# An attention pair on one core: the softmax guard from Gram matrices, and linear attention's K and V as separate jobs

## The chip, the cores and the metric

The kernel runs on one core of one Trainium2 chip. The metric is the device time of one execution in microseconds (us), as the median of several runs; the kernel before was run three times. The profile is of one execution, and its span (761.9 us) is a little shorter than that run's device time (764.1 us).

Engine names in the profile: PE is the matrix engine's multiplications, PEld its weight loads, DVE the vector engine, ACT the scalar engine (which evaluates the exponential), POOL the general-purpose engine, SP the engine that here only issues transfers. L833 is line 833 of the kernel.

## The reference

Two attention blocks with 2048 tokens, width 512 and 32 heads of 16 are computed side by side, each with its own input and weights. A is linear attention, B is full softmax attention. Their outputs are concatenated. All inputs are bf16, drawn from a normal distribution and scaled by 0.05.

```python
qkv = (x @ wqkv).reshape(B, S, 3, H, Dh).transpose(2, 0, 3, 1, 4)   # H = 32, Dh = 16
# A:
phi = lambda t: jnp.where(t > 0, t + 1, jnp.exp(t)) + 1e-6
pq, pk = phi(q), phi(k)
kv  = jnp.einsum("bhsd,bhse->bhde", pk, v);  z = jnp.einsum("bhsd->bhd", pk)
num = jnp.einsum("bhqd,bhde->bhqe", pq, kv)
den = jnp.einsum("bhqd,bhd->bhq", pq, z)[..., None] + 1e-6
a   = (num / den).transpose(0, 2, 1, 3).reshape(B, S, D) @ wo
# B:
scores = jnp.einsum("bhqd,bhkd->bhqk", q, k) * Dh ** -0.5
b   = einsum("bhqk,bhkd->bhqd", softmax(scores), v).transpose(0, 2, 1, 3).reshape(B, S, D) @ wo
out = concatenate([a, b], axis=-1)
```

The exponentials of B are the bulk: 32 heads x 2048 x 2048 scores. The kernel cuts them into 2048 blocks of 128 keys x 512 queries of one head; a block is a tile of 128 partitions x 512 columns.

## The kernel before

Softmax is computed without subtracting a row maximum. A guard bounds the largest score. Only if the bound exceeds a threshold does a second, general program run at the end; with these inputs it does not.

Each score block takes one of two ways. On the ACT way, PE writes three or two blocks into the score banks (`SCR`, tile pS), and one ACT instruction of 1536 or 1024 columns takes the exponential into PT. On the DVE way, PE writes one block into one of the two remaining banks (`DB`, tile pD), DVE turns it into an int16 whose bits are an approximate power of two (tile DI), and for three blocks at a time three more DVE instructions refine it into two factors (DQ and DI). PE then multiplies the exponentials with V and accumulates in pPV: one multiplication for an ACT block, two for a DVE block. 64 blocks (16 key tiles x 4 heads) make a unit, and there are 32 units.

```python
def ex(st_, en_):                                       # the ACT way, w = 1536 or 1024 (L833)
    sch.add("act", lambda e: e.activation(PT[:, row, c0:c0 + w], SCR[sl][:, 0:w], ACTF.Exp, scale=SC), ...)

def p1(st_, en_, ...):                                  # the DVE way, one or two blocks (L773)
    sch.add("dve", lambda e: e.tensor_scalar(DI[:, buf, i * 512:(i + n) * 512], DB[:, bi * 512:(bi + n) * 512],
                                             ESC, EB, op0=ALU.mult, op1=ALU.add), ...)
ops = [                                                 # then, for a group of three (L889, L890, L891)
    (..., lambda e: e.tensor_scalar(Q, I, 0x3FF, 0x3800, op0=ALU.bitwise_and, op1=ALU.bitwise_or), ...),
    (..., lambda e: e.tensor_tensor(Qh, Ih, Qh, op=ALU.mult), ...),
    (..., lambda e: e.tensor_scalar(I, I, 0xFC00, 8, op0=ALU.bitwise_and, op1=ALU.bitwise_or), ...)]
```

Everything else (B's projections, all of A, the output projections) is cut into jobs. A job borrows one of the two DB banks for a PE part, followed by ACT or DVE parts that read that bank. The order of all instructions is fixed while the kernel is built: a planner keeps a clock for each engine and gives each instruction a planned length; whenever the plan shows DVE and a DB bank free, it sends a score block the DVE way, and the ACT way takes the rest. On the chip each engine then works through its list in that order and waits on semaphores.

```python
TEND = 755.0                          # the plan's assumed end; spreads B's and A's jobs over the time
def job_cand():                       # which job may start next
    bi = min((i for i in range(2) if dfree[i] is not None), key=lambda i: dfree[i], default=None)
    ...
    if j_.bank:
        if bi is None: continue       # no DB bank free
```

The parts that the change replaces, shortened:

```python
# guard: largest |q| and |k| of each projection (16 projections of Q, 16 of K)
("dve", 0.6, tensor_reduce(QMX[:, i:i+1], QT[:, r, cs], max, abs))              # L469, in each Q job, 128x512
("dve", 1.14, tensor_reduce(KMX[:, i:i+1], KM[:, r, :, cs], max, abs))          # L476, first K jobs, 128x1024
("dve", 0.6, tensor_reduce(KMX[:, i:i+1], KR[:, kr, :], max, abs))              # L490, other K jobs, 128x512
# bound_job: four small DVE instructions; flag_job: one small PE product and one DVE maximum into FLG

# A's exp part of phi: ACT exp into EA (L546), DVE min/add on EA (L547), DVE max/add with the bank (L549)
def akv_job(t, hp):                   # one token tile, half of the heads: K in columns 0:256, V in 256:512 of one bank
    st = halves(mm, ["Wa", ("xTa", t)], n=8, parts=2, dur=0.14)                 # 8 products of 256 columns
    st += phi_stages(0, 256, KNa[:, t, :], [("KNa", t)])                        # EA 256 wide
    st.append(("dve", 0.33, tensor_copy(VNa[:, t, :, 0:128], bank[:, 256:512])))   # L559
```

Of the kernel before, what the change touches and what calls it, by code (L numbers as in the profile page):

```python
# [123 lines left out]
THRESHOLD_BITS = 0x41140000  # L124
# [99 lines left out]
def bass_concat_heads__linear_attn_block__softmax_full_mha__prompt_kernel(nc, A_x, A_wqkv, A_wo, B_x, B_wqkv, B_wo, out):  # L224
# [3 lines left out]
    NGP = 4  # L228
# [15 lines left out]
    TEND = 755.0  # L244
# [3 lines left out]
    FM = 0.12  # L248
    WARM = (30,)
# [8 lines left out]
    with es:  # L258
# [38 lines left out]
        QMX = sb("QMX", [128, NGP * NC], F32)  # L297
        KMX = sb("KMX", [128, NGP * NC], F32)
        BND = sb("BND", [128, NGP], F32)
        BN1 = sb("BN1", [128, 1], F32)  # L300
# [99 lines left out]
        def push(eng, ready, prio, dur, run):  # L400
            seq[0] += 1
            cands[eng].append((ready, prio, seq[0], dur, run))

        class Job:
# [11 lines left out]
            def stage_done(self, i, end, bk, bi):  # L416
                if i == self.rel and bi is not None:
                    dfree[bi] = end + LAT
                for st, tk in self.gives:
                    if st == i:  # L420
                        tok[tk] = end + LAT
                if i + 1 < len(self.stages):
                    eng, dur, fn = self.stages[i + 1]
                    lat = LAT if eng != "pe" or eng != self.stages[i][0] else 0.0
                    push(eng, end + lat, self.prio if eng == "pe" else (0 if i + 1 <= self.rel and self.bank else min(self.prio, 2)), dur,
                         lambda st_, en_, fn=fn: (fn(bk), self.stage_done(i + 1, en_, bk, bi)))
# [29 lines left out]
        def proj_job(Gp, sc, kind, fast=False, **kw):  # L456
# [10 lines left out]
            if kind == 0:  # L467
                st.append(("dve", 0.6, f_ev("dve", lambda e, bk: e.tensor_copy(QT[:, r, cs], f32v(bk)), [], [("QT", r, sc)])))
                st.append(("dve", 0.6, f_op("dve", lambda e: e.tensor_reduce(QMX[:, i:i + 1], QT[:, r, cs], axis=AX.X, op=ALU.max,  # L469
                                                                             apply_absolute_value=True), [("QT", r, sc)], [("QMX", i)])))  # L470
                return Job(st, needs, [(2, ("Q", Gp, sc)), (3, ("QMX", i))], rel=2, **kw)
            if fast:
                for e_ in range(2):
                    st.append(("dve", 0.67, f_ev("dve", lambda e, bk, e_=e_: e.tensor_scalar(KM[:, r, e_, cs], f32v(bk), PAR[:, e_:e_ + 1], None, op0=ALU.mult),
                                                 [("PAR", e_)], km_keys(r, e_, sc))))
                st.append(("dve", 1.14, f_op("dve", lambda e: e.tensor_reduce(KMX[:, i:i + 1], KM[:, r, :, cs], axis=AX.XY, op=ALU.max,  # L476
                                                                            apply_absolute_value=True),
                                            km_keys(r, 0, sc) + km_keys(r, 1, sc), [("KMX", i)])))
                return Job(st, needs, [(2, ("K", Gp, 0, sc)), (3, ("K", Gp, 1, sc)), (4, ("KMX", i))], rel=3, **kw)
# [3 lines left out]
            def spread(bk):  # L483
                for e_ in range(2):
                    for g in range(4):
# [4 lines left out]
            st.append(("dve", 0.6, f_op("dve", lambda e: e.tensor_reduce(KMX[:, i:i + 1], KR[:, kr, :], axis=AX.X, op=ALU.max,  # L490
                                                                         apply_absolute_value=True), [("KR", kr)], [("KMX", i)])))
            return Job(st, needs, [(3, ("K", Gp, 0, sc)), (3, ("K", Gp, 1, sc)), (4, ("KMX", i))], rel=2, **kw)

        def bound_job(**kw):
            n = NGP * NC
            return Job([
                ("dve", 0.2, f_op("dve", lambda e: e.tensor_reduce(BND[:, 0:NGP], QMX[:].rearrange("p (g s) -> p g s", s=NC), axis=AX.X, op=ALU.max),
                                  [("QMX", i) for i in range(n)], ["BND"])),
                ("dve", 0.2, f_op("dve", lambda e: e.tensor_reduce(KMX[:, 0:NGP], KMX[:].rearrange("p (g s) -> p g s", s=NC), axis=AX.X, op=ALU.max),
                                  [("KMX", i) for i in range(n)], [("KMX", i) for i in range(n)])),  # L500
                ("dve", 0.2, f_op("dve", lambda e: e.scalar_tensor_tensor(BND[:], BND[:], SC, KMX[:, 0:NGP], op0=ALU.mult, op1=ALU.mult),
                                  ["BND"] + [("KMX", i) for i in range(n)], ["BND"])),
                ("dve", 0.2, f_op("dve", lambda e: e.tensor_reduce(BN1[:], BND[:], axis=AX.X, op=ALU.max), ["BND"], ["BN1"])),
            ], [("QMX", i) for i in range(n)] + [("KMX", i) for i in range(n)], [(3, "BN1")], bank=False, **kw)

        def flag_job(**kw):
            return Job([
                ("pe", 0.3, f_pe(lambda e, bk: e.matmul(bk[0][0:1, bk[2]:bk[2] + 128], lhsT=BN1[:], rhs=BMk[:], start=True, stop=True), ["BN1", "BMk"])),
                ("dve", 0.3, f_ev("dve", lambda e, bk: e.tensor_reduce(FLG[:], bk[0][0:1, bk[2]:bk[2] + 128], axis=AX.X, op=ALU.max), [], ["FLG"]))],
                ["BN1"], [], **kw)  # L510

# [40 lines left out]
        def akv_job(t, hp, **kw):  # L552
            def mm(e, bk, i):
                k_, cc = divmod(i, 4)
                return e.matmul(f32v(bk)[:, 256 * k_:256 * k_ + 256], lhsT=xTa[:, cc, t * 128:(t + 1) * 128],  # L555
                                rhs=Wa[:, cc, 512 + 512 * k_ + 256 * hp:512 + 512 * k_ + 256 * hp + 256], start=(cc == 0), stop=(cc == 3))
            st = halves(mm, ["Wa", ("xTa", t)], n=8, parts=2, dur=0.14)
            st += phi_stages(0, 256, KNa[:, t, :], [("KNa", t)])
            st.append(("dve", 0.33, f_ev("dve", lambda e, bk: e.tensor_copy(VNa[:, t, :, 0:128], f32v(bk)[:, 256:512].rearrange("p (b n) -> p b n", n=128)),  # L559
                                        [], [("VNa", t)])))  # L560
            return Job(st, [("xTa", t)] + ([("akv", hp - 1, bl) for bl in range(2)] if hp else []),
                       [(5, ("ak", hp, t))], **kw)

        def akvsum_job(hp, bl, **kw):
# [7 lines left out]
            return Job(st, [("ak", hp, t) for t in range(NT)], [(3, ("akv", hp, bl)), (5, ("rha", bq))], **kw)  # L572
# [120 lines left out]

        afree = [0.0, 0.0]
# [16 lines left out]
        def d_backlog(at):  # L711

            w = max(0.0, T["dve"] - at) + sum(c_[3] for c_ in cands["dve"])
            for s_ in dgroup["st"].values():
                if not s_.get("chained"):
                    w += 1.0 * len(s_["items"])
# [27 lines left out]
        def d_take(pk):  # L744
# [3 lines left out]
            if not dgroup["open"]:  # L748
# [4 lines left out]
                dgroup["st"][buf] = {"p1": 0, "closed": False, "items": []}  # L753
            s_ = dgroup["st"][buf]
            i = len(s_["items"])
            s_["items"].append(b)
            dgleft[buf] += 1
            if len(s_["items"]) == DG:
                s_["closed"] = True
                dgroup["open"] = False  # L760
            return b, buf, bi, i

        def d_emit(tk, en):

            for b, buf, bi, i in tk:
                bk = DBANK[bi]
                sch.add("pe", lambda e, bk=bk, b=b: qk(e, f32v(bk), b), reads=qk_reads([b]), writes=[bk[3]])
            pair = len(tk) == 2 and tk[0][1] == tk[1][1] and tk[0][2] == 0 and tk[1][2] == 1
            for part in ([tk] if pair else [[x] for x in tk]):
                n = len(part)  # L770
                _, buf, bi, i = part[0]
                def p1(st_, en_, part=part, n=n, buf=buf, bi=bi, i=i):
                    sch.add("dve", lambda e: e.tensor_scalar(DI[:, buf, i * 512:(i + n) * 512], DB[:, bi * 512:(bi + n) * 512],  # L773
                                                             ESC, EB, op0=ALU.mult, op1=ALU.add),
                            reads=[("D", bi + x) for x in range(n)], writes=[("DI", buf, i + x) for x in range(n)])
                    for x in range(n):
                        dfree[bi + x] = en_ + LAT
                    s_ = dgroup["st"][buf]
                    s_["p1"] += n
                    s_["t"] = en_  # L780
                    chain(buf)
                push("dve", en + LAT, 0, 0.065 + 0.535 * n, p1)
# [3 lines left out]
        def fill_act_cand():  # L786
# [19 lines left out]
            def run(st, en):  # L806
# [16 lines left out]
                if tk:  # L823
                    tk.sort(key=lambda x: x[3])
# [16 lines left out]
        def fill_d_cand():  # L841
# [11 lines left out]
            def run(st, en):  # L853
# [4 lines left out]
                tk.sort(key=lambda x: x[3])  # L858
# [9 lines left out]
        def chain(buf):  # L868
            s_ = dgroup["st"][buf]
            if not s_["closed"] or s_["p1"] < len(s_["items"]):  # L870
# [213 lines left out]
        for e_ in range(2):  # L1084
            for j, t_ in enumerate((6.6, 8.5, 9.3)):
# [5 lines left out]
        kmx = ("dve", 1.14, f_op("dve", lambda e: e.tensor_reduce(KMX[:, 0:1], KM[:, 0, :, 0:512], axis=AX.XY, op=ALU.max, apply_absolute_value=True),  # L1091
                                 km_keys(0, 0, 0) + km_keys(0, 1, 0), [("KMX", 0)]))
        qmx = ("dve", 0.6, f_op("dve", lambda e: e.tensor_reduce(QMX[:, 0:1], QT[:, 0, 0:512], axis=AX.X, op=ALU.max, apply_absolute_value=True),
                                [("QT0", i) for i in range(2)], [("QMX", 0)]))
        urgent, urgent2, early, bjobs, ajobs = [], [], [], [], []
        urgent2.append(Job([kmx], gives=[(0, ("KMX", 0))], bank=False, ready=30.0))
        urgent2.append(Job([qmx], gives=[(0, ("QMX", 0))], bank=False, ready=30.0))

# [16 lines left out]
        bjobs.append(bound_job(ready=0))  # L1115
        bjobs.append(flag_job(ready=0))
        aout_job = lambda t: omm_job("a", t, 4 + t % 2, [("aont", t)], [(1, ("aout", t))])
        for hp in range(2):
            for t in range(NT):
                ajobs.append(akv_job(t, hp))  # L1120
# [15 lines left out]
        def job_cand():  # L1136
            best = None
            bi = min((i for i in range(2) if dfree[i] is not None), key=lambda i: dfree[i], default=None)
            for lst, pr in ((urgent, 0.5), (early, 2), (bjobs, 2.2), (urgent2, 2.3), (ajobs, 2.5)):
                for pos, j_ in enumerate(lst[:1] if lst is not urgent2 else lst[:8]):  # L1140
# [4 lines left out]
                    if j_.bank:  # L1145
                        if bi is None:
# [3 lines left out]
                    if best is None or (st, pr) < (best[0], best[1]):  # L1150
                        def run(st_, en_, j_=j_, lst=lst, fn=fn):
                            lst.remove(j_)
                            bk, b_ = (DBANK[bi], bi) if j_.bank else (None, None)
                            if j_.bank:
                                dfree[bi] = None
                            fn(bk)
# [164 lines left out]
```

## Time and profile before

| | |
|---|---|
| device time, median of 3 | 765.7 us (764.09 to 766.62) |
| span of the profiled execution | 761.9 us |
| ACT busy | 745.3 us (98%), 695 instructions |
| DVE busy | 721.9 us (95%), 1287 instructions |
| PE busy | 688.9 us (90%), of which 114.3 us products of L1181 that only fill pauses |
| PE clock granted, mean | 0.997 of full speed |
| blocks on the ACT way / the DVE way | 1603 / 445 |

The counts of blocks are those of the products into pS and pD on L682. "Busy" is the time in which at least one instruction of an engine is under way; since the end of one instruction overlaps the start of the next, counts times mean length come to more than the busy time. The planner's lengths in the code are assumptions of the kernel's author, and no measurement.

### The profile page before, as it was taken

What the parts mean: (1) busy time and instruction counts of PE and PEld (TensorE: products, weight loads), DVE (VectorE), ACT (ScalarE), POOL (GpSimd) and SP (SyncE); (2) the same over time, 40 slices, a digit from 0 to 9 for tenths busy, and PEclk for the clock granted to TensorE, in tenths of its full rate; (3) what the DMA queues carried; (4) which work ended last, traced back from release to release, by engine and by line L of the source; (5) the groups of instructions that cost most, each with busy time, mean ns of one, the idle gap of its engine ahead of it and who ended that gap; (6) DMA issues with size and microseconds to landing.
All of it is one profiled execution on the core that took longest, in us unless ns stands there. A gap on an engine that the chain in (4) does not pass through costs nothing.

```text
span 761.9 us, 14767 instructions
## 1 busy us (share of the span) xinstructions
PE 688.9 (90%) x6181; PEld 238.0 (31%) x6232; DVE 721.9 (95%) x1287; ACT 745.3 (98%) x695; POOL 8.6 (1%) x27
## 2 busy tenths in 40 slices
PE   8889999998999998999888899998998989899896
PEld 4223333333333333333222333222323232223232
DVE  5999979999999999999999999999999999999993
ACT  6999999999999999999999999999999999999995
POOL 4000000000000000000000000000000000000000
PEclk9999999999999999999999999999999999999999
DMA  9900000000000000000010000000010001010001
GB/s 216 226 1 2 1 1 8 15 9 2 1 1 2 1 1 2 9 14 8 22 22 8 1 10 21 22 19 11 16 28 15 9 1 43 22 36 22 22 8 33
DMA packets 36570, 17.29 MB, mean 23 GB/s; under 512 B 27536, under 2 KB 35984, under 8 KB 36496
## 3 DMA queue, kind: packets, MB, share of 16 engines
q1 hardware_dynamic: 35408, 15.61, 8.4%
q8 instruction: 51, 0.84, 0.5%
q10 hardware_dynamic: 1088, 0.66, 0.3%
q14 instruction: 23, 0.19, 0.1%
HBM read 4.46 MB, written 4.19 MB: 11 GB/s over the span
## 4 chain that ended last, share of the span: by engine, by line
ACT 96%; PE 2%; DMA 1%; SPq 0%; issue 0%; DVE 0%; DVEq 0%; ACTq 0%
ACT PT L833 94%; ACT EA L546 2%; DMA Wb<-in_B_wqkv_dram 1%; PE pS L1013 0%; PE pPV L1181 0%; PE pS L682 0%; PE pPV L961 0%; SPq L332 0%; ACT KNa L440 0%; PE pS L1055 0%; PE pD L1055 0%; DVEq L1265 0%; DVE DI L773 0%; PE pD L1181 0%; PE pD L576 0%
## 5 line engine op out<-in xcount | busy, mean ns | idle before, releaser
L833 ACT ACTIVATE PT<-pS 128x1536 f16<-128x1536 f32 (+1 forms) x641 | 740.0, 1488 | 1.8 <-PE pS L682 1.0
L773 DVE TENSOR_SCALAR DI<-pD 128x512 int16<-128x512 f32 (+1 forms) x435 | 296.6, 694 | 10.0 <-PE pD L682 8.0
L682 PE MATMUL pS<-QT,KM 32*128 32x512 bf16 x1603 | 249.9, 385 | 49.3 <-ACT PT L833 36.1
L961 PE MATMUL pPV<-PT,VV 128*17 128x512 f16 x1603 | 209.8, 383 | 0.7 <-ACT PT L833 0.7
L682 PE MATMUL pD<-QT,KM 32*128 32x512 bf16 x445 | 161.1, 385 | 1.0 <-DVE PQT L549 0.6
L682 PEld LDWEIGHTS pS<-QT,KM 32*128 32x128 bf16 x1603 | 61.2, 91 | 272.9 <-ACT PT L833 257.8
L890 DVE TENSOR_TENSOR DQ<-DI,DQ 128x1536 f16<-128x1536 f16 x149 | 140.8, 945 | 1.2
L1181 PE MATMUL pPV<-xTb,ZW 128*17 128x256 bf16 x729 | 114.3, 275 | 0.0
L961 PE MATMUL pPV<-DQ,VV 128*17 128x512 f16 x445 | 99.8, 382 | 1.5 <-DVE OT L988 1.4
L961 PE MATMUL pPV<-DI,VV 128*17 128x512 f16 x445 | 98.6, 379 | 0.3 <-DVE DI L891 0.2
L889 DVE TENSOR_SCALAR DQ<-DI 128x1536 int16<-128x1536 int16 x149 | 81.5, 547 | 1.0
L891 DVE TENSOR_SCALAR DI<-DI 128x1536 int16<-128x1536 int16 x149 | 81.3, 546 | 0.7
L1181 PEld LDWEIGHTS pPV<-xTb,ZW 128*17 128x17 bf16 x729 | 57.6, 91 | 47.3 <-issue 31.5
L961 PEld LDWEIGHTS pPV<-PT,VV 128*17 128x17 bf16 x1603 | 45.2, 88 | 73.3 <-issue 62.3
L682 PEld LDWEIGHTS pD<-QT,KM 32*128 32x128 bf16 x445 | 38.2, 90 | 12.8 <-issue 4.1
L555 PE MATMUL pD<-Wa,xTa 128*128 128x256 bf16 x256 | 38.2, 275 | 0.3
L546 ACT ACTIVATE EA<-pD 128x256 bf16<-128x256 f32 (+1 forms) x48 | 35.3, 735 | 0.0
L458 PE MATMUL pD<-xTb,Wb 128*128 128x512 bf16 x98 | 29.6, 382 | 4.2 <-issue 2.2
L961 PEld LDWEIGHTS pPV<-DQ,VV 128*17 128x17 bf16 x445 | 21.9, 88 | 24.6 <-issue 19.2
L961 PEld LDWEIGHTS pPV<-DI,VV 128*17 128x17 bf16 x445 | 25.6, 89 | 8.1 <-DVE DI L891 2.4
L988 DVE STREAM_TRANSPOSE OT<-pPV 128x512 f32<-128x512 f32 x32 | 22.6, 707 | 4.6 <-PE pPV L961 4.6
L555 PEld LDWEIGHTS pD<-Wa,xTa 128*128 128x128 bf16 x256 | 20.3, 97 | 16.4 <-issue 8.4
(90 smaller groups left out, 331.0 us busy)
## 6 DMA issues: line engine op xcount, KB each, us to landing
out_dram<-KNa SPq DMA_DIRECT2D x30, 128.0 KB, 1.7
Wa<-in_A_wqkv_dram SPq DMA_DIRECT2D x1, 1536.0 KB, 7.9
KM<-KR SPq DMA_DIRECT2D x96, 16.0 KB, 1.8
Wb<-in_B_wqkv_dram SPq DMA_DIRECT2D x2, 384.0 KB, 4.6
Wb<-in_B_wqkv_dram SPq DMA_DIRECT2D x1, 512.0 KB, 4.3
WOb<-in_B_wo_dram SPq DMA_DIRECT2D x1, 512.0 KB, 8.7
WOa<-in_A_wo_dram SPq DMA_DIRECT2D x1, 512.0 KB, 9.5
ON<-in_B_x_dram ACTq DMA_DIRECT2D x1, 256.0 KB, 2.9
```

The source lines that it names most:

```text
L458: return e.matmul(f32v(bk), lhsT=Wb[:, cc, kind * 512 + Gp * 128:kind * 512 + Gp * 128 + 128], rhs=xTb[:, cc, sc * 512:(sc + 1) * 512], st ...
L546: ("act", 0.06 + n * 0.000833, f_ev("act", lambda e, bk: e.activation(EA[:, q, 0:n], f32v(bk)[:, c0:c0 + n], ACTF.Exp), [], [("EA", q)])),
L555: return e.matmul(f32v(bk)[:, 256 * k_:256 * k_ + 256], lhsT=xTa[:, cc, t * 128:(t + 1) * 128], rhs=Wa[:, cc, 512 + 512 * k_ + 256 * hp:51 ...
L682: return e.matmul(dst, lhsT=KM[32 * g:32 * g + 32, Gp % 2, e_, j * 128:(j + 1) * 128], rhs=QT[32 * g:32 * g + 32, Gp % 2, c * 512:(c + 1) ...
L773: sch.add("dve", lambda e: e.tensor_scalar(DI[:, buf, i * 512:(i + n) * 512], DB[:, bi * 512:(bi + n) * 512], ESC, EB, op0=ALU.mult, op1=A ...
L833: sch.add("act", lambda e: e.activation(PT[:, row, c0:c0 + w], SCR[sl][:, 0:w], ACTF.Exp, scale=SC), reads=skeys(sl), writes=[("PT", row, ...
L889: (0.06 + w * 0.00026, lambda e: e.tensor_scalar(Q, I, 0x3FF, 0x3800, op0=ALU.bitwise_and, op1=ALU.bitwise_or), ik, qk_),
L890: (0.08 + w * 0.00052, lambda e: e.tensor_tensor(Qh, Ih, Qh, op=ALU.mult), ik + qk_, qk_),
L891: (0.06 + w * 0.00026, lambda e: e.tensor_scalar(I, I, 0xFC00, 8, op0=ALU.bitwise_and, op1=ALU.bitwise_or), ik, ik)]
L961: sch.add("pe", lambda e, g=g, j=j, h=h, P=P, first=first, last_=last_: e.matmul(PVb[32 * g:32 * g + 17, 0:512], lhsT=VV[:, j, vcol(h):vco ...
L988: sch.add("dve", lambda e: e.transpose(OT[:, 0, :], PVb[:, 0:512]), reads=[("PV", g) for g in range(4)], writes=[("OT", 0)])
L1181: ins = e.matmul(dst, lhsT=ZW[:, 0:17], rhs=xTb[:, 0, 0:256], start=first, stop=first, tile_position=(0, 32 * g))
```

## The change

It has three parts.

The first replaces the guard. By the Cauchy-Schwarz inequality a score is at most a quarter of the product of the lengths of q and k; q is x times a 512x16 slice of the weights, so its squared length is at most the squared length of the token times the largest eigenvalue of the slice's 16x16 Gram matrix, which in turn is at most that matrix's largest absolute row sum. So the new guard takes the Gram matrices of x in tiles of 128 tokens (their largest entry is the largest squared token length) and of the Q and K weights, and needs no reductions of Q and K at all. The threshold is restated for the squared bound: 36.8 squared, which is 1354, in place of 9.25.

The second splits `akv_job`: one job makes K for two token tiles, a second makes V for two, so that the ACT and DVE instructions behind them are 512 columns wide rather than 256.

The third is in the planner. `JB` lets a job take a DB bank only when no other job holds the second one, so that the DVE way always keeps a bank. Two DVE-way blocks are joined into one 1024-column instruction when both are waiting at the moment DVE is planned to take one, and not only when they were issued together. `TEND` falls from 755 to 735.

```diff
-THRESHOLD_BITS = 0x41140000
+THRESHOLD_BITS = 0x44A947AE
...
-    TEND = 755.0
+    TEND = 735.0
+    JB = True
...
                 st.append(("dve", 0.6, f_ev("dve", lambda e, bk: e.tensor_copy(QT[:, r, cs], f32v(bk)), [], [("QT", r, sc)])))
-                st.append(("dve", 0.6, f_op("dve", lambda e: e.tensor_reduce(QMX[:, i:i + 1], QT[:, r, cs], ...))))
...
-                st.append(("dve", 1.14, f_op("dve", lambda e: e.tensor_reduce(KMX[:, i:i + 1], KM[:, r, :, cs], ...))))
...
-            st.append(("dve", 0.6, f_op("dve", lambda e: e.tensor_reduce(KMX[:, i:i + 1], KR[:, kr, :], ...))))
-        def bound_job(**kw): ...
+        def gram_x(t4, **kw):
+                for tl in range(4):
+                    t = 4 * t4 + tl
+                    for cc in range(4):
+                        ins = e.matmul(f32v(bk)[:, tl * 128:(tl + 1) * 128], lhsT=xTb[:, cc, t * 128:(t + 1) * 128], rhs=xTb[:, cc, t * 128:(t + 1) * 128],
+                                       start=(cc == 0), stop=(cc == 3))
+            return Job([("pe", 1.1, ...),
+                        ("dve", 0.6, ... e.tensor_reduce(GRX[:, t4:t4 + 1], f32v(bk), axis=AX.X, op=ALU.max) ...)], ...)
+        def gram_w(kind, **kw):
+                for Gp in range(NGP):
+                    for cc in range(4):
+                        w = Wb[:, cc, kind * 512 + Gp * 128:kind * 512 + Gp * 128 + 128]
+                        ins = e.matmul(f32v(bk)[:, Gp * 128:(Gp + 1) * 128], lhsT=w, rhs=w, start=(cc == 0), stop=(cc == 3))
+            return Job([("pe", 1.1, ...),
+                        ("dve", 0.6, ... e.tensor_reduce(GRW[:, kind, :], f32v(bk).rearrange("p (h c) -> p h c", c=16), op=ALU.add, abs) ...),
+                        ("dve", 0.15, ... GRW times ZMk ...), ("dve", 0.15, ... e.tensor_reduce(TOP[:, 1 + kind:2 + kind], GRW[:, kind, :], op=ALU.max) ...)], ...)
         def flag_job(**kw):
+            # one DVE maximum of GRX, three small PE products with identf, one DVE maximum, two 1x1 DVE products into FLG
...
-        def akv_job(t, hp, **kw): ...
+        def akv_mm(t2, hp, kind):
+                return e.matmul(f32v(bk)[:, 256 * tt:256 * tt + 256], lhsT=xTa[:, cc, (t2 + tt) * 128:(t2 + tt + 1) * 128],
+                                rhs=Wa[:, cc, 512 * kind + 256 * hp:512 * kind + 256 * hp + 256], start=(cc == 0), stop=(cc == 3))
+        def ak_job(t2, hp, **kw):
+            st = akv_mm(t2, hp, 1) + phi_stages(0, 512, KNa[:, t2:t2 + 2, :].rearrange("p a n -> p (a n)"), ...)
+        def av_job(t2, hp, **kw):
+            st = akv_mm(t2, hp, 2)
+            st.append(("dve", 0.6, f_ev("dve", lambda e, bk: e.tensor_copy(VNa[:, t2:t2 + 2, :, 0:128], f32v(bk).rearrange("p (a b n) -> p a b n", a=2, b=2)), ...)))
...
-            pair = len(tk) == 2 and tk[0][1] == tk[1][1] and tk[0][2] == 0 and tk[1][2] == 1
+                    o = waiting.get(1 - bi)
+                    if o is not None and o[0] == buf and o[2][0] <= st_ + 0.02:      # the other bank waits too: one instruction for both
+                        cands["dve"].remove(o[2])
+                        bis = [0, 1]
...
-        bjobs.append(bound_job(ready=0))
-        bjobs.append(flag_job(ready=0))
+        bjobs += [gram_x(i, ready=0) for i in range(4)] + [gram_w(i, ready=0) for i in range(2)] + [flag_job(ready=0)]
...
-            for t in range(NT):
-                ajobs.append(akv_job(t, hp))
+            for t in range(0, NT, 2):
+                ajobs += [ak_job(t, hp), av_job(t, hp)]
...
-                        if bi is None:
+                        if bi is None or (JB and held[1 - bi] and lst is not early):
                             continue
```

## The prediction

> **What bounds the kernel now.** I read the busy shares first, then the chain that ended last, then ACT's own waits, and last the pace at which ACT works. The page's first part and the engine line of its chain:
>
> ```profile
> PE 688.9 (90%) x6181; PEld 238.0 (31%) x6232; DVE 721.9 (95%) x1287; ACT 745.3 (98%) x695; POOL 8.6 (1%) x27
> ACT 96%; PE 2%; DMA 1%; SPq 0%; issue 0%; DVE 0%; DVEq 0%; ACTq 0%
> ```
>
> Two engines are nearly full, but the chain of work back from the end runs over ACT for 96% of the span and over DVE for none of it. So the question is whether ACT ever waits. The waits of ACT, all of them:
>
> ```profile
> ACT KNa L440 <- PE pS L1013: 4.1, 1, 4.1
> ACT xTb L440 <- PE pS L1044: 2.0, 1, 2.0
> ACT L363 <- PEq L1306: 1.8, 1, 1.8
> ACT QT L1065 <- PE pS L1055: 1.4, 1, 1.4
> ACT PT L833 <- PE pS L682: 1.0, 1, 1.0
> ACT PT L833 <- PE pD L682: 0.7, 2, 0.5
> ACT KNa L440 <- ACT KNa L440: 0.5, 1, 0.5
> ```
>
> The columns are total us, times, longest. Apart from the 0.7 us these belong to the start, before the first exponential at 8.74 us, or to the end, after the last at 751.20 us. I asked for the busy times of just that stretch (the pairs are busy us and instructions, in the order PE, PEld, DVE, ACT, POOL):
>
> ```profile
> 8.74:751.20 742.46, 677.82 (x6096) 230.25 (x6144) 715.64 (x1270) 741.67 (x689) 0.94 (x4) 1.00 0.08 21
> ```
>
> ACT is busy for 741.67 of 742.46 us. A wait that the change removes from PE or DVE therefore buys nothing by itself. Time comes only from fewer columns or fewer instructions on ACT, or is lost by making ACT wait.
>
> **What one ACT instruction costs.** By shape:
>
> ```profile
> L833 ACT ACTIVATE PT<-pS 128x1536 f16<-128x1536 f32 x321 | 545.4, 1699 | 1.8 <-PE pS L682 1.0 <-PE pD L682 0.7
> L833 ACT ACTIVATE PT<-pS 128x1024 f16<-128x1024 f32 x320 | 408.2, 1276 | 0.0
> L546 ACT ACTIVATE EA<-pD 128x256 bf16<-128x256 f32 x32 | 21.4, 669 | 0.0
> L546 ACT ACTIVATE EA<-pD 128x512 bf16<-128x512 f32 x16 | 13.9, 867 | 0.0
> ```
>
> The means can't be added: 545.4 + 408.2 is 953.6 us in a span of 762, because instructions overlap. The difference of the two means gives about 0.83 ns per column (423 ns over 512 columns), the overlap has to come from a run of them:
>
> ```profile
> 733.67 17.53 ACT L833 ACTIVATE PT<-pS 128x1536 f16<-128x1536 f32 x15
> ```
>
> These are 15 in alternation, 1536 first and last. The last starts 1.70 us before the end, so 14 starts take 15.83 us for 7 x 2560 = 17920 columns. At 0.833 ns a column that is 14.93 us, and 0.90 us over, or 64 ns for each instruction. The whole stretch gives the same: 321 x 1536 + 320 x 1024 + 32 x 256 + 16 x 512 = 837,120 columns are 697.6 us at 0.833 ns; 741.67 less 0.36 (the tail of the last one) less 697.6, over 689 instructions, is 63 ns. So I use 0.833 ns a column and 64 ns an instruction.
>
> **What the Trainium skill says.** "ScalarE: Activation LUTs", section "What ACT_TABLE_LOAD costs", has an ACTIVATE with immediate operands at 186 ns + 0.833 ns a column, with back-to-back ones overlapping by about 93 ns, so some 93 ns an instruction beyond the columns. The slope agrees with the trace; the fixed part is smaller here, 63 to 64 ns, and I use the trace's. "VectorE: DVE Perf Modes", section "The perf-mode tier table", lets tensor_reduce run only at one element a cycle from any source. The trace agrees: the 512-column reduction of bf16 from SBUF (L469) takes 679 ns, no less than the 684 ns of a copy of 512 f32 columns out of PSUM (L482). So the old guard's reductions were dear, and the new ones out of PSUM should cost the same each. "PSUM — Partial Sum Buffer", section "Engine vs sequencer instructions", says that the ACT and DVE queues are strictly first in, first out. That is the way in which a change that frees DVE could still hurt: an ACT instruction put into ACT's list too early blocks all the exponentials behind it. Before, L546 shows 0.0 us of idle time in both shapes.
>
> **The change part by part.** The order is fixed at build time, so I counted the instructions in the changed kernel's built lists, by engine and shape, against those of before.
>
> ACT, the engine that matters. Blocks on the ACT way fall from 1603 to 1592 and on the DVE way rise from 445 to 456. The 1536-column exponentials go from 321 to 318, the 1024-column ones from 320 to 319: 3 x 1536 + 1024 = 5632 columns less, 4.69 us. The A side has the same 16,384 columns, now as 32 instructions of 512 in place of 32 of 256 and 16 of 512. Together 689 instructions become 669: 20 x 64 ns = 1.28 us. Sum: 6.0 us less on ACT.
>
> DVE, by mean durations, which overstate a little because of the same overlap. Removed with the old guard: 15 x 679 + 674 ns, 12 x 676 ns, 3 x 1215 + 1206 ns, and five small ones at about 160 ns (L499 took 161, L501 156): 24.6 us. A's K and V: before 32 x (218 + 416 + 416) = 33.6 us for L547, L549 and L559 at 256 columns; after 16 x (288 + 682 + 684) = 26.5 us, taking L547 and L549 at 512 columns and L482's copy for the third: 7.1 us less. Added by the new guard: six reductions of 512 columns at 0.68 us, one of 384 at about 0.55 (L521's length) and seven small ones at 0.16: 5.8 us. The 11 more blocks: single DI instructions go from 425 to 428, joined ones from 10 to 14: 3 x 682 + 4 x 1211 ns = 6.9 us; the chains of three go from 148 to 151, at 549 + 949 + 548 ns, plus one chain of two at some 1.5 us, my estimate between the lengths at one and three: 7.6 us. Net: -24.6 - 7.1 + 5.8 + 6.9 + 7.6 = -11.4 us. DVE gives up more than ACT, so it should stay the second engine: about 710 of 756 us.
>
> PE gets 96 products of 128 columns for the Gram matrices. Products of that shape on L530 ran 8 in 0.62 us at 220 ns each, so 57 ns from start to start: 5.5 us. 11 more blocks on the DVE way add 11 products with V, at most 11 x 0.38 = 4.2 us. The fillers of L1181 fall from 743 to 629. At some 0.11 us each (five took 0.71 us near the end, one alone 0.27) that is 12.5 us less. Nothing of this lies on the path while ACT stays fed. The transfers have the same number and sizes.
>
> The start up to the first exponential is unchanged in the lists: the first reduction taken out stood behind the fourth K projection. At the end the last exponential has 1024 columns where it had 1536, which the sum already holds; then come the same last products, normalization and four stores. So the span after the last exponential should stay near the 10.7 us of before.
>
> Sum: 765.7 - 6.0 = 759.7 us, 0.8% less.
>
> **The rivals.** One: ACT starts to wait. Six bursts of 16 Gram products, about 16 x 57 ns = 0.9 us each, stand unsplit in PE's list, and a burst just when score banks come free would hold back the next exponential. For it: PE works in order. Against it: PE waits for ACT far more than ACT for PE (257.8 us of weight loads on L682 wait for an exponential), the bursts of the same kind before (L588, 16 products) cost ACT nothing, and ACT computes 0.9 to 1.3 us on the other buffer meanwhile. If each burst cost 0.5 us, the time were 763.
>
> Two: DVE takes over as bound. The 11 blocks moved to it are worth 14.5 us there. If the planner overloads a stage, PE would stop at a DB bank, and exponentials would starve behind it. For it: DVE is 95% busy, and in some 50 us windows 49.7 of 50. Against it: DVE's sum falls by 11.4 us while ACT's falls by 6.0, and the blocks are spread: counted between the ends of units, each gets 11 to 18 on the DVE way but for the last. If DVE did bind throughout, the gain would shrink towards nothing: 764 to 766.
>
> Three: the freed DVE time turns into more than the counts show, by fewer pauses elsewhere. The 25 us of the old guard look like 25 us of gain, and the lower TEND suggests that its author hoped for 20. Against it: 0.79 us of ACT idle time is all there is to win. The counts fix the rest; anything below 758 would need ACT to run faster per instruction.
>
> Four: the new guard trips, and the general program runs. The bound for these inputs is about 13.5 (largest squared token length 1.52, row sums 2.39 and 2.44) against 1354, so no.
>
> **Range and chances.** The ACT sum is good to a few tenths of a us; the median of three runs before has a spread of 764.1 to 766.6; a few new waits on ACT may add 1 to 2 us. I take 757.0 to 763.0. Faster by over 2% means under 750.4, which needs 9 us that no row offers: 0.02. Slower by over 2% means above 781: 0.02, for a planner's order that starves ACT. Within 2%: 0.96.
>
> **What would show it.** Right: 637 exponentials on ACT, ACT busy near 739 us, its idle time between first and last exponential still about 1 us, DVE busy near 710, and the stretch between first and last exponential near 736.5. Wrong: new waits of ACT for PE's pS or pD of several us (rival one), or long waits of PE for DVE's DI with ACT idle behind them (rival two), or another pace of ACT per column.

## The result, and the profile after

| | before | after |
|---|---|---|
| device time, median of 4 runs each | 764.89 us (763.49 to 766.62) | 760.39 us (759.62 to 762.02) |
| ratio, with 95% interval | | 0.9943 (0.9915 to 0.9971) |
| span of the profiled execution | 761.9 us | 758.5 us |
| ACT busy / DVE busy | 745.3 / 721.9 us | 739.8 / 716.1 us |
| exponentials on ACT, 1536 and 1024 columns | 321 and 320 | 318 and 319 |
| PE clock, mean over runs | 0.997 (86 runs, beside the experiments) | 0.993 (4 runs) |

The change is worth 0.6% (0.3 to 0.9% by the interval). 759.7 us was predicted, with 757.0 to 763.0 as the range. The busy line of the page after, and the engine line of its chain of work that ended last:

```profile
PE 695.9 (92%) x6229; PEld 234.4 (31%) x6229; DVE 716.1 (94%) x1235; ACT 739.8 (98%) x675; POOL 8.5 (1%) x27
ACT 94%; PE 4%; DVE 1%; DMA 1%; SPq 0%; issue 0%; ACTq 0%
```

ACT is busy 5.5 us less, but PE and DVE now have 5% of the chain, where they had 2%. The groups of ACT by shape say why:

```profile
L869 ACT ACTIVATE PT<-pS 128x1536 f16<-128x1536 f32 x318 | 538.6, 1694 | 3.3 <-PE pS L712 2.2 <-PE pD L712 1.1
L869 ACT ACTIVATE PT<-pS 128x1024 f16<-128x1024 f32 x319 | 404.9, 1271 | 1.7 <-PE pD L712 1.7
L571 ACT ACTIVATE EA<-pD 128x512 bf16<-128x512 f32 x32 | 27.3, 854 | 0.0
```

The counts and the mean lengths are as expected. New is the idle time ahead of the exponentials: 5.0 us, of which 1.05 is the start, where before there was 1.8. The stretch from the first exponential to the last, taken in the same way as before (busy us in the order PE, PEld, DVE, ACT, POOL):

```profile
8.59:748.74 740.15, 685.01 (x6144) 226.82 (x6142) 709.87 (x1218) 736.12 (x669) 1.07 (x5) 1.00 0.08 21
```

It is 2.3 us shorter than the 742.46 of before. ACT works 736.1 us in it, where 735.7 was expected (the 741.7 of before less the columns and instructions saved), and doesn't work for 4.0 us, where it was 0.8. So the saving on ACT arrived, and in this execution over half of it was given back as waits. Where they are, by the list of ACT's instructions in order of time (start, length, idle time before the row and its releaser), around 274 us:

```profile
274.00 1.02 ACT L869 ACTIVATE PT<-pS 128x1024 f16<-128x1024 f32 x1 [0.38 <-PE pD L712]
275.94 1.45 ACT L869 ACTIVATE PT<-pS 128x1536 f16<-128x1536 f32 x1 [0.92 <-PE pS L712]
277.93 1.02 ACT L869 ACTIVATE PT<-pS 128x1024 f16<-128x1024 f32 x1 [0.54 <-PE pD L712]
```

Three waits in a row, 1.84 us. The busy times of 3.4 us windows around them show the clock (the first figure after POOL's pair):

```profile
264.20:267.60 3.40, 3.15 (x29) 1.13 (x27) 3.40 (x6) 3.40 (x5) 0.00 (x0) 1.00 0.00 0
267.60:271.00 3.40, 2.50 (x18) 0.66 (x15) 3.40 (x6) 3.40 (x5) 0.00 (x0) 0.98 0.00 0
271.00:274.40 3.40, 2.98 (x27) 0.71 (x30) 2.55 (x7) 3.02 (x4) 0.00 (x0) 0.50 0.02 5
274.40:277.80 3.40, 3.40 (x23) 0.79 (x15) 2.29 (x3) 2.07 (x2) 0.00 (x0) 0.51 0.00 0
277.80:281.20 3.40, 3.40 (x36) 1.68 (x33) 3.23 (x7) 3.27 (x4) 0.00 (x0) 1.00 0.00 0
```

After a window in which PE had little to do (18 products, 2.50 of 3.40 us), its clock stood at half for 6.8 us. PE, busy for 6.4 of these, fed ACT late. Before, the profile has one such stretch, of 3.4 us, and waits of 0.50 and 0.12 us in it and just behind it. The other waits of after are at 24.41, 34.79, 634.36 and 686.70 us (0.81, 0.32, 0.80 and 0.26 us), at full clock. This is the order of time on PE, PEld and DVE ahead of the first of them:

```profile
22.26 1.04 PE L462 MATMUL pD<-xTb,Wb 128*128 128x512 bf16 x4
22.59 0.55 DVE L926 TENSOR_SCALAR DI<-DI 128x1536 int16<-128x1536 int16 x1
23.22 0.09 PEld L996 LDWEIGHTS pPV<-PT,VV 128*17 128x17 bf16 x1 [0.42 <-DVE DI L926]
23.98 0.39 PE L712 MATMUL pS<-QT,KM 32*128 32x512 bf16 x2
24.41 2.37 ACT L869 ACTIVATE PT<-pS 128x1024 f16<-128x1024 f32 x2 [0.81 <-PE pD L712]
```

(Rows between these are left out here.) In PE's list a projection and a batch of V products stand ahead of the two score products that ACT needs. The batch also waits for the last step of a DVE chain, which ends at 23.14 us, but the projection keeps PE at work until 23.30, so DVE costs PE about 0.1 us here at most: from 22.26 to 24.40 us PE is busy all the time. ACT has finished at 23.60 us, and the score products start only at 23.98. The waits at 634 and 687 us were not followed back.

The new guard's own instructions cost what was expected of them: the reductions out of PSUM take 684 to 686 ns.

```profile
L501 DVE TENSOR_REDUCE GRX<-pD 128x1 f32<-128x512 f32 x4 | 2.7, 686 | 0.0
L513 DVE TENSOR_REDUCE GRW<-pD 128x32 f32<-128x512 f32 x2 | 1.4, 684 | 0.0
```

### The profile page after: what moved, and what is told of

Same layout as the page of the kernel before. It is cut to its first block, busy times and chain, and to the rows that moved or that the text cites. A ratio compares the mean times of both kernels' runs of the same rounds, so it can differ in the third digit from the quotient of the medians.

```text
span 758.5 us, 14741 instructions
## 1 busy us (share of the span) xinstructions
PE 695.9 (92%) x6229; PEld 234.4 (31%) x6229; DVE 716.1 (94%) x1235; ACT 739.8 (98%) x675; POOL 8.5 (1%) x27
## 4 chain that ended last, share of the span: by engine, by line
ACT 94%; PE 4%; DVE 1%; DMA 1%; SPq 0%; issue 0%; ACTq 0%
ACT PT L869 91%; ACT EA L571 2%; PE pPV L996 1%; PE pS L712 1%; DMA Wb<-in_B_wqkv_dram 1%; PE pS L1048 0%; PE pD L462 0%; DVE DI L811 0%; DVE DQ L925 0%; SPq L333 0%; ACT KNa L444 0%; DVE KNa L444 0%; PE pPV L1209 0%; PE pS L1090 0%; PE pD L661 0%
## 5 line engine op out<-in xcount | busy, mean ns | idle before, releaser
L869 ACT ACTIVATE PT<-pS 128x1536 f16<-128x1536 f32 x637 | 732.5, 1482 | 5.1 <-PE pD L712 2.8
L811 DVE TENSOR_SCALAR DI<-pD 128x512 int16<-128x512 f32 (+1 forms) x442 | 304.0, 698 | 18.1 <-PE pD L712 15.9
L996 PE MATMUL pPV<-PT,VV 128*17 128x512 f16 x1592 | 204.7, 384 | 1.2 <-DVE OT L1023 1.2
L712 PE MATMUL pD<-QT,KM 32*128 32x512 bf16 x456 | 169.2, 386 | 0.8 <-issue 0.5
L925 DVE TENSOR_TENSOR DQ<-DI,DQ 128x1536 f16<-128x1536 f16 x153 | 144.1, 942 | 1.6
L996 PE MATMUL pPV<-DI,VV 128*17 128x512 f16 x456 | 101.7, 383 | 0.0
L1209 PE MATMUL pPV<-xTb,ZW 128*17 128x256 bf16 x593 | 93.9, 274 | 0.0
L1209 PEld LDWEIGHTS pPV<-xTb,ZW 128*17 128x17 bf16 x593 | 45.2, 91 | 39.4 <-issue 29.4
L462 PE MATMUL pD<-xTb,Wb 128*128 128x512 bf16 x120 | 34.7, 383 | 1.0 <-DVE DI L811 0.6
L571 ACT ACTIVATE EA<-pD 128x512 bf16<-128x512 f32 x32 | 27.3, 854 | 0.0
```

Of the source, the lines that this page charges most:

```text
L462: return e.matmul(f32v(bk), lhsT=Wb[:, cc, kind * 512 + Gp * 128:kind * 512 + Gp * 128 + 128], rhs=xTb[:, cc, sc * 512:(sc + 1) * 512], st ...
L571: ("act", 0.06 + n * 0.000833, f_ev("act", lambda e, bk: e.activation(EA[:, q, 0:n], f32v(bk)[:, c0:c0 + n], ACTF.Exp), [], [("EA", q)])),
L712: return e.matmul(dst, lhsT=KM[32 * g:32 * g + 32, Gp % 2, e_, j * 128:(j + 1) * 128], rhs=QT[32 * g:32 * g + 32, Gp % 2, c * 512:(c + 1) ...
L925: (0.08 + w * 0.00052, lambda e: e.tensor_tensor(Qh, Ih, Qh, op=ALU.mult), ik + qk_, qk_),
L996: sch.add("pe", lambda e, g=g, j=j, h=h, P=P, first=first, last_=last_: e.matmul(PVb[32 * g:32 * g + 17, 0:512], lhsT=VV[:, j, vcol(h):vco ...
L1209: ins = e.matmul(dst, lhsT=ZW[:, 0:17], rhs=xTb[:, 0, 0:256], start=first, stop=first, tile_position=(0, 32 * g))
```

## The experiments

Two theories of the time were put to the test, and two of ACT's waits. The ACT theory: the time is ACT's columns and instructions, plus ACT's waits, and DVE time is worth nothing for itself. The DVE theory: DVE at 95% is as good as the bound, and freed DVE time is freed time. For the waits: the clock (PE's pauses halve its clock), and the planner's order.

**The old guard left out, nothing else moved.**

```diff
# kernel before, at each of the guard's reductions
-  ("dve", 0.6, f_op("dve", lambda e: e.tensor_reduce(QMX[...] ...)))
+  ("dve", 0.6, lambda bk: None)        # keeps its place in the plan, executes nothing; FLG is set to 0
```

> The kernel before with the old guard's 32 large reductions and its five small DVE instructions left out, the order of everything else unchanged (the flag is set to zero). ACT theory: the columns and instructions on ACT are the same, so the time stays within 1 us of the kernel before (about 764.9), and DVE's busy time falls by some 22 to 25 us into idle time. DVE theory: time follows DVE, so it falls by 10 to 25 us, to 740 to 755.

Measured: 763.57 us, ratio 0.9997 (0.9983 to 1.0011). In its stretch between first and last exponential DVE is busy for 698.0 us, 17.6 less than before, and the time has not moved.

```profile
8.48:750.11 741.63, 675.74 (x6094) 229.53 (x6142) 698.00 (x1234) 741.46 (x689) 1.20 (x5) 1.00 0.08 21
```

The DVE theory falls. The guard's reductions were free where they stood. What a cheaper guard can bring is only what the planner makes of the room.

**The guard, the split and the planner's part, each alone.** Each is the kernel before with that part of the change and a new plan.

```diff
+ gram_x, gram_w, flag_job; no QMX, KMX, bound_job      # guard alone
+ ak_job, av_job in place of akv_job                    # split alone
+ JB = True, joining in d_emit, TEND = 735.0            # planner alone
```

> The new guard alone on the kernel before, planned anew. ACT theory: 833,536 columns in 687 instructions, against 837,120 in 689: 3.1 us less, about 761.8, plus whatever new waits ACT has. DVE theory: DVE gives up 24.6 us and gets 5.8 us and seven blocks (about 9.5 us) back, so 9 us less, about 756.

> A's K and V as separate jobs alone. ACT theory: 836,608 columns in 673 instructions: 1.5 us less, about 763.4. DVE theory: 7.1 us less on DVE and one block more (1.4 us): about 759.

> The planner's part alone (a job takes a bank only if no other job holds the second, joining of blocks, TEND 735). ACT theory: 837,632 columns in 690 instructions: 0.5 us more, about 765.4. If the bank rule keeps PE and ACT better fed on the chip, ACT's waits are fewer than the 0.8 us of before, which can bring at most that. If its order costs ACT waits, they show as several us for PE's pD or pS: 767 to 769.

Measured: the guard 1.0009 (0.9996 to 1.0022), the split 0.9964 (0.9952 to 0.9975), the planner's part 1.0001 (0.9989 to 1.0013). The whole change has 0.9943. The guard, which frees most DVE time, brings nothing alone. ACT is busy for the 738.9 us that its count gives, but doesn't work for 2.7 us of the stretch, with the waits at 24.45 and 34.84 us that the changed kernel has too, and its 22 runs have a mean clock of 0.992 where the kernel before has 0.997. The split brings more than the 1.5 us of the count (about 3 us by the medians, 763.82 and 760.87); where the rest comes from isn't shown.

**Guard and split together, without the planner's part.**

```diff
  # kernel before + gram_x, gram_w, flag_job + ak_job, av_job; TEND stays at 755, no JB, joining as before
```

> The new guard and the split of K and V together, without the planner's part: 832,000 columns in 669 instructions on ACT, 5.6 us less than before, 0.4 more than the changed kernel. By the ACT sum a ratio of 0.993; if the two parts' own results add (1.0009 and 0.9964), 0.997; if the planner's part is what spares waits, slower than the changed kernel by over 1 us (0.996 or more).

Measured: 759.44 us, ratio 0.9942 (0.9928 to 0.9956), the changed kernel's own ratio. So the planner's part adds nothing that these runs can show, alone or on top.

```profile
8.19:746.35 738.16, 675.84 (x6117) 230.23 (x6166) 707.28 (x1219) 736.22 (x669) 1.35 (x6) 1.00 0.08 21
```

This stretch has no half clock in it, and the mean clock of the six runs is 0.997, as before. ACT still doesn't work for 1.9 us of it, 1.1 more than before, and the early waits (0.81 and 0.32 us, at 24.0 and 34.4 us) are that much.

**The Gram products left out of the changed kernel, nothing else moved.**

```diff
-  Job([("pe", 1.1, f_pe(f, ...)), ("dve", 0.6, ...)], ...)
+  Job([("pe", 1.1, lambda bk: None), ("dve", 0.6, lambda bk: None)], ...)     # FLG is set to 0
```

> The changed kernel with the new guard's Gram products and DVE instructions left out, the order of everything else unchanged (the flag is set to zero). If the bursts of 16 Gram products hold exponentials back, the time falls by 1 to 3 us against the changed kernel (760.4, ratio 0.9943 to before), to a ratio of 0.990 to 0.993. If they lie beside ACT's work, it stays within 0.5 us: 0.9937 to 0.995. The early waits of ACT at 24.4 and 34.8 us, which have no Gram product near them, stay in both cases.

Measured: 762.45 us, ratio 0.9974 (0.9960 to 0.9988). Neither expectation: with less to do it is not faster, and by the points slower, though the interval just overlaps that of the changed kernel, which did not run beside it. The mean clock of its 14 runs is 0.986, against 0.993. Its profile has 17.1 us at half clock, 10.2 of them from 557 to 568 us, where four of the six Gram bursts had stood in whole or in part. The same windows in this run and in the changed kernel:

```profile
557.00:568.00 11.00, 10.53 (x72) 1.98 (x73) 7.57 (x13) 10.12 (x10) 0.00 (x0) 0.53 0.00 1
```

```profile
557.00:568.00 11.00, 9.95 (x123) 4.31 (x121) 11.00 (x20) 11.00 (x12) 0.00 (x0) 1.00 0.01 2
```

72 products at half clock against 123 at full clock, and ACT idle for 0.9 us. The waits at 24.3 and 34.7 us stayed, as expected. In this order the Gram bursts do not hold ACT back: they stand between 541.57 and 568.85 us, and the changed kernel's profile has no wait of ACT from 278 to 634 us. From 557 to 568 us they do the fillers' work.

**No fillers, and more fillers.** The order is the changed kernel's in both.

```diff
 def fill_in(st):
-    if n <= 0:
+    if True:          # no fillers
         return
```

```diff
-    FM = 0.12
+    FM = 0.05         # 834 fillers for 629
```

> The changed kernel without any of the products that fill PE's pauses (629 left out), everything else in the same order. Clock theory (PE's pauses bring its clock down to half, and at half clock PE feeds ACT late): many half-clock stretches, mean clock below 0.95, ACT waits of over 10 us, ratio to before above 1.005. Order theory (waits come only from where the planner put things): ACT's waits stay at some 3 us, ratio 0.993 to 0.996.

> The changed kernel with 834 fillers in place of 629 (pauses filled up to 0.05 us rather than to 0.12), everything else in the same order. Clock theory: fewer half-clock stretches than the 6.8 us of the changed kernel's profile and 0.5 to 2 us less time, ratio 0.9915 to 0.9935. Order theory: no change, or slower by up to 1 us where a filler stands before the products that ACT waits for.

Measured: without fillers 781.28 us, ratio 1.0217 (1.0194 to 1.0241). PE's clock in the 40 slices of its page, and ACT's waits:

```profile
PEclk9979999999998989998899899998999889899888
```

```profile
ACT PT L869 <- PE pD L712: 15.0, 24, 1.3
ACT PT L869 <- PE pS L712: 6.6, 13, 1.0
```

```profile
8.35:770.25 761.90, 646.69 (x5521) 185.04 (x5519) 711.72 (x1218) 740.75 (x669) 1.30 (x5) 0.93 0.08 20
```

The stretch has 105.8 us at half clock, in 21 pieces, and is 21.75 us longer than the changed kernel's, so 0.22 us lost for each of the 99.0 us more at half clock. By that rate the 6.8 us of the changed kernel's profile cost 1.5 us, near the 1.84 us of waits seen in and just behind them. With 834 fillers the ratio is 0.9948 (0.9928 to 0.9969): no gain, though the mean clock of its six runs is 0.996. Its profile, of the run with the lowest clock of the six (0.991), still has 10.2 us at half clock. The fillers stand where the plan has pauses; the pause of 0.95 us at 270 us is there with 834 fillers too, so the plan seems not to have it.

**The early order of before, in the changed kernel.**

```diff
             # first K jobs
+            st.append(("dve", 1.14, lambda bk: None))     # the old reduction's place in the plan, not executed
```

> The changed kernel with the planned time of the old guard's three early reductions (1.14 us each on DVE, not executed) kept in the plan. ACT has the same 831,488 columns in 669 instructions, and the first 60 rows of PE's list are those of the kernel before. If the early waits come from the order that fills DVE where the reductions stood, the waits at 24.4 and 34.8 us (1.13 us idle, and about 0.7 of lost overlap) go away: 1 to 2 us less than the changed kernel, ratio 0.992 to 0.993. If they only move elsewhere in the plan, the ratio stays at 0.994 to 0.995.

Measured: 760.41 us, ratio 0.9956 (0.9942 to 0.9971). The waits at 24.4 and 34.8 us are gone, as expected, and others have come, at 155.14 us (0.81) and 617.04 us (0.92) among them. The second expectation holds, a little above its range but within the noise: the waits move.

**The old reductions twice.**

```diff
-  e.tensor_reduce(QMX[:, i:i+1], QT[:, r, cs], ...)
+  e.tensor_reduce(QM2[:, i:i+1], QT[:, r, cs], ...); e.tensor_reduce(QMX[:, i:i+1], QT[:, r, cs], ...)
```

> The kernel before with 30 of the old guard's 32 large reductions executed twice, in the same order: some 22 us more on DVE, nothing more on ACT. If ACT alone binds and DVE has slack at every place, the time stays at a ratio of 1.000 to 1.002. If DVE is as good as full where the reductions stand (120 to 170, 300 to 345, 490 to 560 us), the planned order makes PE and then ACT wait: 1.005 to 1.02. Full DVE-bound would be 1.029.

Measured: 777.66 us, ratio 1.0186 (1.0163 to 1.0209). Some 22 us more on DVE by mean lengths, 16.6 us of busy time in the stretch, cost 14 us, as the second expectation had it, while taking that work away brought nothing that the runs can show. The waits of ACT in this run:

```profile
ACT PT L832 <- PE pS L681: 7.8, 14, 1.2
ACT PT L832 <- PE pD L681: 2.6, 9, 0.7
```

They are put down to PE, because PE stands between: it stops at a bank that DVE has not yet emptied, and the score products stand behind it in its list. PE's idle time that DVE ends is 30.3 us in this run, and 9.5 before. The largest part of it in this run stands ahead of B's projections. First that wait in the kernel before, then in this run:

```profile
PE pD L458 <- DVE DI L773: 1.2, 4, 0.5
```

```profile
PE pD L460 <- DVE DI L772: 6.6, 12, 1.2
```

DVE doesn't bind before, but there is little room to it. Part of the cost is the clock, at half for 10.2 us.

**Two other settings of the planner, in the changed kernel.**

```diff
-    DLEAD = 0.5, PVR = 3
+    DLEAD = 1.0, PVR = 2                              # the first
```

```diff
-    TEND = 735.0, DEND = 20, PVR = 3, PVO = 16
+    TEND = 750.0, DEND = 12, PVR = 2, PVO = 20        # the second
```

> The changed kernel with the planner looking for DVE-way blocks earlier (DLEAD 1.0 for 0.5) and cutting V products into smaller batches (PVR 2 for 3): 465 blocks on the DVE way, 826,880 columns in 665 instructions on ACT, 462 fillers. ACT sum alone: 4.1 us less than the changed kernel, ratio to before 0.988 to 0.990. With waits: DVE is fuller and there are 167 fillers fewer, so more half-clock stretches; if they eat the gain, 0.992 to 0.996.

> Another setting of the planner (TEND 750, DEND 12, PVR 2, PVO 20): 464 blocks on the DVE way, 827,392 columns in 666 instructions on ACT, 605 fillers. ACT sum: 3.6 us less than the changed kernel, ratio 0.989 to 0.991 if its waits are like those of the changed kernel. It has nearly the fillers of the changed kernel, so under the clock theory it should beat the setting with 462 fillers in spite of 0.5 us more on ACT.

Measured: 756.07 us, ratio 0.9889 (0.9873 to 0.9905), and 754.67 us, ratio 0.9869 (0.9852 to 0.9887). Both beat both kernels. The second, with half a us more on ACT, is the faster in the profile by its waits:

```profile
8.57:742.62 734.05, 672.55 (x6076) 224.49 (x6121) 714.95 (x1234) 732.41 (x666) 1.08 (x5) 1.00 0.09 21
```

ACT doesn't work for 1.6 us of it, against 3.7 in the first, and it has 3.4 us at half clock against 6.8. In the first, 2.07 us of waits lie at 23.98 and 37.17 us, at full clock. So the fillers' number alone doesn't explain the difference. Against the kernel before, the second gains 9.3 us by the medians, where the count gives 9.6.

All runs together. "ACT by count" is the 741.7 us of before, less 0.833 ns for each column and 64 ns for each instruction fewer in the lists; the times at half clock are those between the first and the last exponential:

| kernel | ACT by count | ACT busy in its stretch | stretch less busy | half clock in the profile | ratio to before |
|---|---|---|---|---|---|
| before | 741.7 | 741.7 | 0.8 | 3.4 | 1 |
| old guard left out | 741.7 | 741.5 | 0.2 | 0 | 0.9997 |
| guard | 738.6 | 738.9 | 2.7 | 3.4 | 1.0009 |
| split | 740.2 | 740.2 | 0.5 | 3.4 | 0.9964 |
| planner | 742.2 | 742.2 | 1.6 | 6.8 | 1.0001 |
| guard and split | 736.1 | 736.2 | 1.9 | 0 | 0.9942 |
| after | 735.7 | 736.1 | 4.0 | 6.8 | 0.9943 |
| after, Gram products left out | 735.7 | 736.5 | 3.8 | 17.1 | 0.9974 |
| after, early order | 735.7 | 736.1 | 3.5 | 3.4 | 0.9956 |
| after, more fillers | 735.7 | 736.3 | 4.5 | 10.2 | 0.9948 |
| after, DLEAD and PVR | 731.6 | 732.3 | 3.7 | 6.8 | 0.9889 |
| after, four settings | 732.1 | 732.4 | 1.6 | 3.4 | 0.9869 |
| after, no fillers | 735.7 | 740.8 | 21.2 | 105.8 | 1.0217 |
| before, reductions twice | 741.7 | 745.7 | 11.4 | 10.2 | 1.0186 |

The ratio is of all runs; ACT's busy time, the rest of the stretch and the half clock are of one profiled execution, which is not always a typical one (the planner's, 767.5 us, is the slowest of its 14 runs). Where there are many waits, ACT's busy time grows too (740.8 against 736.1 us for the same list), which fits that an exponential before a wait has nothing to overlap with.

## Why the prediction was right

The time lies in the range, 0.7 us above the point. That it is so close is partly luck: the working started from 765.7 us, and the kernel before has a median of 764.9 with a fourth run, so the 6.0 us would have led to 758.9. Step by step:

- ACT is the bound, and DVE time brings nothing by itself: shown. Leaving out the guard's 32 reductions moved nothing. That only columns and instructions on ACT bring time is not shown in full: the split brought about 1.5 us more than its count.
- 6.0 us from 5632 columns and 20 instructions: shown for ACT's work. Its busy time in the stretch fell by 5.5 us, and the count meets the busy time within 0.8 us in every kernel whose ACT has few waits.
- DVE at about 710 us: it is 716.1 on the page, 5.8 us less where 11.4 was said. The working said that mean durations overstate; by the run that leaves the old guard out, its 24.6 us are 17.6 us of busy time.
- "its idle time between first and last exponential still about 1 us": this failed. It is 4.0 us in the profile. The range had 1 to 2 us for new waits; the profile has 3.2 more than before, of which 1.84 in one stretch at half clock, which the prediction did not consider, though its own count had the fillers fall from 743 to 629.
- Rival one named the Gram bursts. They did not delay ACT; from 557 to 568 us they kept the clock up, and without them the kernel is no faster. But what it describes, PE busy with other products when ACT needs scores, is what the wait at 24.4 us is, with a projection and V products in the place of the Gram products. Two of its reasons against were weak: the bursts of L588 are products of 8 columns, not of 128, and the 257.8 us are idle time of the weight loads, while PE itself is idle for ACT for 36.1 us on L682 (page of before). Rival two, that PE stops at DVE and the exponentials starve behind, did not come with the change; the doubled reductions show it.
- The start and the end: 9.8 us from the last exponential to the end of the span, where 10.7 was said.

By the medians the gain is 4.5 us, so 1.5 us of the 6.0 are missing; the interval of four runs each allows gains of 2.2 to 6.5 us. The clock would account for much of that, by an estimate: over the runs of one kernel time goes with its mean clock: for the kernel before, 23 runs at 0.999 have a median of 763.2 us and 28 runs at 0.995 one of 764.5, 0.3 us for 0.001. The changed kernel's runs stand 0.004 lower than that kernel's, which would be 1.2 us. But three kernels with a mean clock of 0.996 to 0.997, near that of before, gain no more: more fillers (0.9948), the early order (0.9956), guard and split (0.9942). The last of these gains 4.6 of the 5.6 us of its count, with 1.1 us more waits than before, and none of them at half clock. So waits that a new order brings at full clock are enough for a shortfall of this size. How that of the changed kernel divides between the clock and the planner's waits isn't settled: the order decides when PE pauses, and so both.

## What to carry to other kernels

Where one engine is busy for 99.9% of the stretch that counts, the gain of a change is the work that it takes off that engine, counted from the instruction lists, less the waits that a new order brings; work taken off the second engine is worth only what a planner moves into the room, and may be worth nothing, while the same work added there can cost most of its length. When a plan is made anew, look at the first engine's waits and at PE's clock before praising or blaming the parts of the change: here four settings of the planner were worth about as much on top of the change (0.9869 against 0.9943) as the change itself. Leaving an instruction out while its place in the plan stays is the experiment that separates an instruction's own cost from the effect of a new order; on PE it also takes away work that may have kept the clock up, as the Gram products showed.

## What the runs showed of the hardware

In the changed kernel's profile PE's clock fell to half after a window that was only thinly filled, not idle: 2.50 of 3.40 us busy, the longest pause 0.95 us, which was still under way when it fell. The Trainium skill, "TensorE: Matmul & The Clock Gate", section "HAM oscillation — how this bites in real kernels", gives "no PE-idle gaps >~3.4µs" as the rule. The traces differ from it: here the clock fell with no pause near that length. How thin a window must be isn't settled: from 547.38 to 550.79 us of the same execution PE was busy for 2.30 of 3.41 us, and the clock stayed at full. All 40 stretches at half clock between first and last exponential in the 14 profiles last 3.4 us, or two or three times that (6.8 at 271 us here, 10.2 at 557 us without the Gram products).

Products without use are worth 2.7% of the time before here (1.0217 without them, 0.9943 with them), and useful ones can do the same: from 557 to 568 us the clock is 1.00 with the Gram products and 0.53 without.

A microsecond of PE at half clock cost about 0.22 us of the time here, by the run without fillers.
